# Eight tokens of each partition in one stored row: x blocks that step over a pair of chunks

## The chip, the core and the metric

The kernel runs on one core of a Trainium2 chip. The core has a matrix engine (PE), a vector engine (DVE), an activation engine (ACT), a general engine (POOL) and an engine that only issues transfers (SP); 16 DMA engines carry the traffic between HBM and the on-chip memory SBUF. The metric is device time in microseconds (us). The kernel before took 203.31 us, the median of two runs (203.01 and 203.61).

## What is computed

A linear recurrence runs along each of 8 sequences of 6400 tokens, 128 features wide; its output x is then put through a mixture of rank-16 adapters with two of eight experts chosen for each token. All in float32:

```python
# a, b: (8, 6400, 128); w_gate (128, 8); A (8, 128, 16); B (8, 16, 128)
for t in range(S):
    h = a[:, t] * h + b[:, t]
    x[:, t] = h
x = x.reshape(51200, 128)
logits = x @ w_gate
w = softmax(two largest logits of each token)
delta[n] = sum over the two experts e of w[n, e] * ((x[n] @ A[e]) @ B[e])
out = x + delta
```

## The kernel before

The 51,200 tokens are cut into 100 chunks of 512. The features lie along the 128 partitions while the recurrence runs, the tokens while loading, gating and storing.

**Front, for each chunk.** Loads of a and b bring two chunks at a time (512 KB, tiles `a_tm` and `b_tm`), eight tokens in a row of 4 KB in each partition; only the first four chunks are loaded one by one. Of such a pair, partitions 0 to 63 hold the first chunk, 64 to 127 the second. PE transposes them into `pA` and `pB` (line 728), groups of 16 small matmuls called `P`; ACT copies `pA` to `a_st` (L746); DVE runs the recurrence over the chunk with one scan instruction (L784) and writes x in half precision into a slot of `xT`, features by 512 tokens. There are NX = 24 slots, used in turn.

**Logits and adapters.** A block is 128 tokens. Four blocks make a chunk: block j of a chunk holds its columns j, j+4, j+8 and so on, which `xblock` (L665) gives as a view of the slot, so that the token of partition p and block j is token 4p + j of the chunk. Units of six blocks, one and a half chunks, (of four at the head and the tail; 69 in all) go through PE at L804: each block of x is loaded as the weights, and the gate and all A stream past it, into `pZ`. ACT copies a unit to `zl` (L810). A group of up to four units is gated on DVE and POOL (L841 to L880).

**Back, for each chunk.** POOL (for a few chunks DVE) multiplies the adapter inputs by the gate (L913), PE transposes the product (L926), ACT or DVE copies it to `zwT` (L932, L935), and PE adds x and the adapters' output in PSUM: L940 loads a block of x as weights and multiplies by the identity, L941 adds the product with B. These eight matmuls are the op `D`. ACT or DVE copies the result into `outt` (L955, L952), a ring of 72 blocks.

**Stores.** Two chunks at a time go out as one transfer of 512 KB (L986): each partition sends two rows of 2 KB, four tokens of the one chunk and four of the other. The last four chunks are stored one by one. The store that begins with chunk 68 is issued in two pieces, 124 partitions and 4.

**What sets the order.** Every piece of work is an op with an engine, a list of ops that it depends on, and a place. `schedule` (L330) puts the ops of each engine in order of a rank, made of a base and a number written out by hand for each op (`NUDGE`, L30). With `WINDOW` at 0 for each engine only the first op of its queue can be next, so the ranks are the order. `waits` (L400) turns the dependencies into semaphore waits ahead of the instructions. An engine carries out its list as it stands, and one that waits holds up all behind it.

The dependencies that the change touches: the logits op of a unit depends on the scan of the chunk in which its last block lies (`c1`, L797 and L807); the scan of a chunk depends on the last reader of its slot of `xT`, the op `D` of chunk c - 24 (`xlast`, L792 and L945); the fronts needed by a unit are created before it (L1020).

Of the kernel before, what the change touches and what calls it, by code (L numbers as in the profile page):

```python
# [8 lines left out]
F16 = mybir.dt.float16  # L9
# [226 lines left out]
NX = 24  # L236
# [207 lines left out]
def bass_associative_scan_2x2__then__mixture_of_adapters_kernel(  # L444
# [13 lines left out]
    C = 512  # L458
    J = C // 128
# [10 lines left out]
    b0 = 0  # L470
# [4 lines left out]
    NU = len(units)  # L475

    GMAX = 4
    stores = []
    c0 = 0
    for n in [2] * ((NCH - sum(STORE_TAIL)) // 2) + STORE_TAIL:  # L480
        stores.append((c0, n))
        c0 += n
    assert c0 == NCH

# [33 lines left out]
    with ExitStack() as stack:  # L518
        sb = stack.enter_context

        def sbuf(name, shape, dt, n=None):
            if n is None:
                return sb(nc.sbuf_tensor(name, shape, dt))
            return [sb(nc.sbuf_tensor(f"{name}{i}", shape, dt)) for i in range(n)]
# [20 lines left out]
        a_tm = sbuf("a_tm", [128, HC * J, D], F32, NL)  # L545
        b_tm = sbuf("b_tm", [128, HC * J, D], F32, NL)
        a_st = sbuf("a_st", [128, C], F32, NA)
        xT = sbuf("xT", [128, C], F16, NX)
        zl = sbuf("zl", [128, NZ, W], F32)
        zw = sbuf("zw", [128, J, 128], F16, NW)  # L550
        zwT = sbuf("zwT", [128, C], F16, NW)
        outt = sbuf("outt", [128, NO, 128], F32)
# [23 lines left out]
        def dma_sem(key):  # L576
            if key not in s_dma:
# [7 lines left out]
                out=ident_f[:, :], in_=ident_f[:, :], compare_op=ALU.not_equal, fill=1.0,  # L585
# [32 lines left out]
        def place_pick():  # L618
            with nc.allow_low_precision(reason="sums of a single one"):
# [8 lines left out]
                out=own[:, :], in_=ident_f[:, :].rearrange("q (e h) -> q e h", e=E),  # L628
# [6 lines left out]
                out=spread[:, :, :].rearrange("q l (e r) -> q l e r", e=E),  # L635
# [19 lines left out]
        o_Z, o_ze, o_mu, o_T, o_te, o_D, o_oe, o_st = {}, {}, {}, {}, {}, {}, {}, {}  # L655
        o_g = {}
        zlast, xlast, olast = {}, {}, {}

        def get(d, k):
            return [(d[k], True)] if k in d else []  # L660

        def xcols(c):
            return xT[c % NX][:, :]

        def xblock(b):  # L665
            return xcols(b // J).rearrange("d (p j) -> d j p", j=J)[:, b % J, :]

        def te_act(c):
            return c in TE_ACT
# [1 line left out]
        def fr(c, kind):  # L671
            if c < HEAD:
                return (EARLY + 2 * c + (kind == "B"), "", 0)
            return (PERIOD * (c // PERIOD), kind, c % PERIOD)
# [14 lines left out]
        def woven(c):  # L689
            return HEAD <= c < NCH - TAIL and c // HC not in FLAT  # L690
# [32 lines left out]
        def trans(*which):  # L723
            def f():
                lists = [pieces(*w) for w in which]
                for group in zip(*lists):
                    for args in group:
                        last = eng["pe"].transpose(*args)  # L728
                return last
            return f  # L730

        def part_a(c):
            return (c, a_tm, pA[:, c % 2, :])
# [4 lines left out]
        def deps_a(c):  # L738
            return [(o_la[c], True), (o_id, True)] + get(o_ae, c - 2)
# [8 lines left out]
        def front(c):  # L748
            r0 = rows[c]
            o_fi = []  # L750
            for k in range(FILL.get(c, 0)):
                o_fi.append((P.add(
                    "pe", f"fi{c}_{k}", 0.109, [(o_id, True)] + get(o_sc, c - 2),
                    lambda: eng["pe"].transpose(pB[:, c % 2, 0:128], ident_f[:, :], ident_f[:, :]), fr(c, "fi")), True))
            if not woven(c):
                o_A[c] = P.add("pe", f"A{c}", 0.109 * J, deps_a(c), trans(part_a(c)), fr(c, "A"))
                o_B[c] = P.add("pe", f"B{c}", 0.109 * J, deps_b(c) + o_fi, trans(part_b(c)), fr(c, "B"))
                add_ae(c)
            elif c % 2 == 0:
                if c not in o_A:  # L760
                    o_A[c] = P.add("pe", f"A{c}", HALVES, deps_a(c), trans(part_a(c)), fr(c, "A"))
                    add_ae(c)
                o_A[c + 1] = o_B[c] = P.add("pe", f"P{c}", HALVES, deps_a(c + 1) + deps_b(c) + o_fi,
                                            trans(part_a(c + 1), part_b(c)), fr(c, "B"))
                add_ae(c + 1)
            elif woven(c + 1):
                load_next(c + 1)
                o_A[c + 1] = o_B[c] = P.add("pe", f"P{c}", HALVES, deps_b(c) + deps_a(c + 1) + o_fi,
                                            trans(part_b(c), part_a(c + 1)), fr(c, "B"))
                add_ae(c + 1)  # L770
            else:
                o_B[c] = P.add("pe", f"B{c}", HALVES, deps_b(c) + o_fi, trans(part_b(c)), fr(c, "B"))

            x = xcols(c)
            starts = sorted({0} | {n * S - r0 for n in range(NB) if 0 < n * S - r0 < C})
            segs = list(zip(starts, starts[1:] + [C]))

            def scan():
                for s0, s1 in segs:
                    if (r0 + s0) % S == 0:  # L780
                        init = 0.0
                    else:
                        init = xcols(c - 1)[:, C - 1 : C]
                    last = eng["dve"].tensor_tensor_scan(  # L784
                        out=x[:, s0:s1], data0=a_st[c % NA][:, s0:s1], data1=pB[:, c % 2, s0:s1],
                        initial=init, op0=ALU.mult, op1=ALU.add,
                    )
                return last

            o_sc[c] = P.add("dve", f"sc{c}", 1.276 + 0.16 * (len(segs) - 1),  # L790
                            [(o_ae[c], True), (o_B[c], True)] + get(o_sc, c - 1)
                            + get(xlast, c % NX),  # L792
                            scan, fr(c, "sc"))

        def zlogits(u):
            b0, n = units[u]
            c1 = (b0 + n - 1) // J  # L797
            zb = zpos[u]
            zold = {zlast[zb + k].i: zlast[zb + k] for k in range(n) if zb + k in zlast}

            def zmm():
                for k in range(n):
                    o = k % (n // 2) * W
                    last = eng["pe"].matmul(pZ[:, k // (n // 2), o : o + W], xblock(b0 + k), Awg_h)  # L804
                return last

            o_Z[u] = P.add("pe", f"Z{u}", 0.11 + 0.059 * n, [(o_sc[c1], True), (o_ch, True), (o_cc, True)] + get(o_ze, u - 1), zmm, un(u, "Z"))  # L807

            def ze():
                return eng["act"].copy(  # L810
                    zl[:, zb : zb + n, :].rearrange("p (h k) w -> p h (k w)", h=2),
                    pZ[:, :, 0 : n // 2 * W])

            o_ze[u] = P.add("act", f"ze{u}", 0.167 + 0.1133 * n, [(o_Z[u], True)] + [(x, True) for x in zold.values()], ze, un(u, "ze"))
# [84 lines left out]
        def back_part(gi, ch, c, b0, n):  # L899
# [42 lines left out]
                return last  # L942

            o_D[c] = P.add("pe", f"D{c}", 0.11 + 0.112 * n, [(o_te[c], True)], delta, ba(gi, c, "D"))
            xlast[ch % NX] = o_D[c]  # L945
            o0 = b0 % NO
            freed = {olast[o0 + k].i: olast[o0 + k] for k in range(n) if o0 + k in olast}
            deps = [(o_D[c], True)] + [(x, True) for x in freed.values()]
# [27 lines left out]
        def store(c, m):  # L976
            q = c * J % NO
            r0 = rows[c]
            src = {olast[q + k].i: olast[q + k] for k in range(m * J)}
            dst = out[r0 : r0 + m * C, :].rearrange("(h p j) d -> p h j d", p=128, j=J)  # L980
            view = outt[:, q : q + m * J, :].rearrange("p (h j) d -> p h j d", j=J)
            cuts = SPLIT.get(c, [128])
            lows = [sum(cuts[:i]) for i in range(len(cuts))]

            def send():
                all = [eng["sp"].dma_start(dst[p : p + n], view[p : p + n]) for p, n in zip(lows, cuts)]  # L986
                return all if len(all) > 1 else all[0]

            op = P.add(
                "sp", f"st{c}", m * C * D * 4 / (STORE_RATE if m == 2 else LOAD_RATE), [(x, True) for x in src.values()],  # L990
                send, (PERIOD * (c // PERIOD), "st", c % PERIOD // 2),
                sem=dma_sem(f"st{q // (2 * J)}" if m == 2 else f"stx{c % 4}"), parts=len(cuts),
            )
            o_st[c] = op
            for k in range(m * J):
                olast[q + k] = op
# [17 lines left out]
                load(c, 1 if c < HEAD else HC)  # L1014

        nf, nb = 0, 0
        for gi, (u0, n) in enumerate(groups):
            for u in range(u0, u0 + n):
                b0, m = units[u]
                while nf * J < b0 + m:  # L1020
                    load_next(nf)
                    front(nf)
                    nf += 1
                zlogits(u)
            gating(gi)
            while (nb + 1) * J <= sum(units[u0 + n - 1]):
                while nb >= NCH - TAIL_CHUNKS and nf < NCH:
                    load_next(nf)
                    front(nf)
                    nf += 1  # L1030
                back(gi, nb)
                nb += 1
# [72 lines left out]
```

## Time and profile before

| | |
|---|---|
| median of the runs | 203.31 us |
| span of the profiled execution, first to last instruction | 200.9 us |
| moved by DMA | 79.26 MB at 395 GB/s, 29065 packets |
| scans on DVE (L784) | 104, of which 96 take 120.4 us |
| logits matmuls on PE (L804) | 400, mean 225 ns |
| x matmuls of the back (L940) | 400 (368 into pO, 16 into pA, 16 into pB) |
| pair stores | 47 of 512 KB, one of 496 KB and 16 KB |

The profile is one execution, recorded on the chip; its own time is known as the span, 200.9 us, which leaves out what lies before the first and after the last instruction. "Busy" is the time in which an engine carried out instructions. Matmuls overlap, and each lasts some 220 ns in the records while the next starts after some 55, so PE's busy time is not a measure of its rate. PEld is the weight loads of PE, which lie beside its matmuls. In groups of instructions a row gives the line, engine and operation, the output and inputs with their shapes, the count, the busy us and the mean ns of one, and then the idle time just before with what ended it. In lists of waits a row says who waited for whom: total us, times, longest. In lists in order of time a row begins with the start and the duration in us.

### The profile page before, as it was taken

The page shows a single profiled execution, that of the slowest core. Times are in us where ns is not written, and L with a number is a line of the kernel's source. Part 1 is how long each engine was busy: PE and PEld are TensorE (multiplying, and loading weights), DVE is VectorE, ACT ScalarE, POOL GpSimd, SP SyncE. Part 2 cuts the span into 40 slices and gives each one's busy share as a digit, 9 for nine tenths or more (in the row PEclk, how much of TensorE's full clock was granted, in tenths as well). Part 3 has the DMA queues.
Part 4 walks back from the last instruction along what each step waited for, and adds up shares of the span by engine and source line. Part 5 has one row for each costly group of instructions (what it writes and reads, how often), then busy time and mean ns, then how long its engine had stood idle before and what let it go on. Part 6 is the DMA issues. An engine that isn't in the chain of part 4 may idle for free.

```text
span 200.9 us, 7611 instructions
## 1 busy us (share of the span) xinstructions
PE 177.7 (88%) x3192; PEld 155.9 (78%) x3192; DVE 176.2 (88%) x283; ACT 175.8 (88%) x327; POOL 136.9 (68%) x176
## 2 busy tenths in 40 slices
PE   6888978999899969999988999899999997898970
PEld 6766867888688858888878888787888886787860
DVE  1699999999999968999897999798899998999971
ACT  2589998999779969999997999899999998899970
POOL 1331559498989887797987797868876466767420
PEclk9999999999999999999999999999999999999998
DMA  6999999999999999999999999999999999999985
GB/s 216 378 412 408 411 405 401 411 406 404 414 409 400 412 416 409 401 417 407 409 413 409 410 409 412 413 410 411 417 408 410 414 410 409 406 381 387 357 338 215
DMA packets 29065, 79.26 MB, mean 395 GB/s; under 512 B 2664, under 2 KB 2920, under 8 KB 29032
## 3 DMA queue, kind: packets, MB, share of 16 engines
q1 hardware_dynamic: 28456, 78.39, 99.0%
q8 instruction: 25, 0.41, 0.8%
q10 hardware_dynamic: 576, 0.40, 0.7%
q14 instruction: 8, 0.07, 0.1%
HBM read 52.56 MB, written 26.21 MB: 392 GB/s over the span
## 4 chain that ended last, share of the span: by engine, by line
DMA 33%; PE 27%; DVE 16%; ACT 15%; SPq 5%; issue 2%; DVEq 0%; ACTq 0%
DMA a_tm<-in_a_dram 26%; DVE xT L784 9%; DMA out_dram<-outt 7%; ACT zl L810 5%; PE pZ L804 5%; SPq L707 5%; PE pB L728 5%; PE pA L728 5%; ACT outt L955 4%; PE pO L940 4%; PE pO L926 4%; ACT a_st L746 4%; PE pO L941 3%; DVE zwT L935 2%; ACT zwT L932 2%
## 5 line engine op out<-in xcount | busy, mean ns | idle before, releaser
L784 DVE TENSOR_TENSOR_SCAN xT<-a_st,xT,pB 128x512 f16<-128x512 f32 x96 | 120.4, 1254 | 7.1 <-PE pA L728 4.3
L913 POOL TENSOR_TENSOR zw<-zl,g 128x512 f16<-128x512 f32 x88 | 92.7, 1067 | 27.9 <-DVE g L880 19.6
L728 PE MATMUL pB<-ident_f,b_tm 64*128 64x64 f32 (+1 forms) x784 | 69.3, 229 | 6.8 <-DMA a_tm<-in_a_dram 6.7
L728 PE MATMUL pA<-ident_f,a_tm 64*128 64x64 f32 (+1 forms) x784 | 69.8, 230 | 0.5 <-DMA b_tm<-in_b_dram 0.3
L746 ACT COPY a_st<-pA 128x512 f32<-128x512 f32 x100 | 63.3, 638 | 4.1 <-PE pA L728 3.3
L728 PEld LDWEIGHTS pB<-ident_f,b_tm 64*128 64x128 f32 (+1 forms) x784 | 56.4, 139 | 11.8 <-DMA a_tm<-in_a_dram 8.3
L810 ACT COPY zl<-pZ 128x816 f32<-128x816 f32 (+1 forms) x69 | 59.7, 865 | 2.0 <-PE pZ L804 1.7
L728 PEld LDWEIGHTS pA<-ident_f,a_tm 64*128 64x128 f32 (+1 forms) x784 | 56.8, 139 | 5.6 <-issue 0.4
L955 ACT COPY outt<-pO 128x512 f32<-128x512 f32 x88 | 55.9, 640 | 3.9 <-PE pO L941 3.0
L940 PE MATMUL pO<-ident_h,xT 128*128 128x128 f16 x368 | 51.6, 222 | 1.3 <-ACT zwT L932 1.0
L941 PE MATMUL pO<-cst_h,zwT 128*128 128x128 f16 x368 | 50.5, 219 | 0.0
L940 PEld LDWEIGHTS pO<-ident_h,xT 128*128 128x128 f16 x368 | 40.2, 113 | 4.3 <-ACT zwT L932 1.4
L804 PE MATMUL pZ<-cst_h,xT 128*128 128x136 f16 x400 | 35.9, 225 | 4.9 <-DVE xT L784 2.0
L941 PEld LDWEIGHTS pO<-cst_h,zwT 128*128 128x128 f16 x368 | 36.8, 100 | 0.0
L926 PE MATMUL pO<-ident_h,zw 128*128 128x128 f16 x368 | 35.2, 220 | 1.4 <-ACT outt L955 1.1
L804 PEld LDWEIGHTS pZ<-cst_h,xT 128*128 128x128 f16 x400 | 26.3, 114 | 9.1 <-DVE xT L784 4.3
L926 PEld LDWEIGHTS pO<-ident_h,zw 128*128 128x128 f16 x368 | 22.9, 97 | 4.7 <-ACT outt L955 1.3
L935 DVE COPY zwT<-pO 128x512 f16<-128x512 f16 x57 | 22.9, 407 | 4.0 <-PE pO L926 3.7
L932 ACT COPY zwT<-pO 128x512 f16<-128x512 f16 x35 | 21.9, 630 | 4.7 <-PE pO L926 4.3
L850 POOL TENSOR_TENSOR L<-k,m 128x192 f32<-128x192 f32 (+2 forms) x16 | 8.4, 524 | 6.2 <-DVE m L848 6.1
L872 POOL TENSOR_TENSOR k<-k,L 128x192 f32<-128x192 f32 (+1 forms) x17 | 9.4, 556 | 4.3 <-DVE L L868 3.0
L846 POOL TENSOR_TENSOR L<-L,k 128x192 f32<-128x192 f32 (+1 forms) x15 | 8.6, 576 | 5.4 <-DVE L L843 4.7
(58 smaller groups left out, 112.2 us busy)
## 6 DMA issues: line engine op xcount, KB each, us to landing
a_tm<-in_a_dram SPq DMA_DIRECT2D x48, 512.0 KB, 13.3
b_tm<-in_b_dram SPq DMA_DIRECT2D x48, 512.0 KB, 13.5
out_dram<-outt SPq DMA_DIRECT2D x47, 512.0 KB, 13.4
a_tm<-in_a_dram SPq DMA_DIRECT2D x4, 256.0 KB, 4.3
out_dram<-outt SPq DMA_DIRECT2D x4, 256.0 KB, 3.6
b_tm<-in_b_dram SPq DMA_DIRECT2D x3, 256.0 KB, 5.1
out_dram<-outt SPq DMA_DIRECT2D x1, 496.0 KB
b_tm<-in_b_dram ACTq DMA_DIRECT2D x1, 256.0 KB, 3.4
```

Of the source, the lines that this page charges most:

```text
L728: last = eng["pe"].transpose(*args)
L746: lambda: eng["act"].copy(a_st[c % NA][:, :], pA[:, c % 2, :]), fr(c, "ae"))
L784: last = eng["dve"].tensor_tensor_scan(out=x[:, s0:s1], data0=a_st[c % NA][:, s0:s1], data1=pB[:, c % 2, s0:s1], initial=init, op0=ALU.mul ...
L804: last = eng["pe"].matmul(pZ[:, k // (n // 2), o : o + W], xblock(b0 + k), Awg_h)
L810: return eng["act"].copy(zl[:, zb : zb + n, :].rearrange("p (h k) w -> p h (k w)", h=2), pZ[:, :, 0 : n // 2 * W])
L913: lambda: eng["pool"].tensor_tensor(out=wv, in0=zv, in1=gv, op=ALU.mult), ba(gi, c, "mu"))
L926: last = eng["pe"].transpose(ptile[:, k * 128 : k * 128 + 128], zz[:, k, :], ident_h[:, :])
L932: lambda: eng["act"].copy(zt, ptile[:, 0 : n * 128]), ba(gi, c, "ta"))
L935: lambda: eng["dve"].tensor_copy(zt, ptile[:, 0 : n * 128]), ba(gi, c, "te"))
L940: eng["pe"].matmul(dst, xblock(b0 + k), ident_h[:, :], start=True, stop=False)
L941: last = eng["pe"].matmul(dst, zt[:, k * 128 : k * 128 + 128], B_h, start=False, stop=True)
L955: lambda: eng["act"].copy(ov, bv), ba(gi, c, "oe"))
```

## The change

Stores of two chunks write one row of eight tokens in each partition: token 8p + k of the pair of chunks, 1024 tokens, is now in partition p and block k of the pair, for k from 0 to 7. So a block takes every eighth column of the two slots of the pair instead of every fourth of one. To make such a view possible the slots of `xT` become one tensor, and `tile_of` records which chunks are stored together. The last four chunks, stored singly, keep their blocks as they were. Since a block now has tokens of both chunks, the logits op of a unit depends on the scan of the last chunk of the pair in which the unit ends; the slots of a pair are free again when both `D` of the pair are done; and the fronts of a whole pair are created before the unit that needs them. The numbers of `NUDGE` are the same.

```diff
-    stores = []
+    stores, tile_of = [], {}
     c0 = 0
     for n in [2] * ((NCH - sum(STORE_TAIL)) // 2) + STORE_TAIL:
         stores.append((c0, n))
+        assert c0 % NX + n <= NX
+        for c in range(c0, c0 + n):
+            tile_of[c] = (c0, n)
         c0 += n
...
-        xT = sbuf("xT", [128, C], F16, NX)
+        xT = sbuf("xT", [128, NX * C], F16)
...
         def xcols(c):
-            return xT[c % NX][:, :]
+            o = c % NX * C
+            return xT[:, o : o + C]
 
         def xblock(b):
-            return xcols(b // J).rearrange("d (p j) -> d j p", j=J)[:, b % J, :]
+            s0, n = tile_of[b // J]
+            o = s0 % NX * C
+            return xT[:, o : o + n * C].rearrange("d (p j) -> d j p", p=128)[:, b - s0 * J, :]
...
                             [(o_ae[c], True), (o_B[c], True)] + get(o_sc, c - 1)
-                            + get(xlast, c % NX),
+                            + xlast.get(c % NX, (0, []))[1],
...
         def zlogits(u):
             b0, n = units[u]
-            c1 = (b0 + n - 1) // J
+            c1 = sum(tile_of[(b0 + n - 1) // J]) - 1
...
-            xlast[ch % NX] = o_D[c]
+            s0, m = tile_of[ch]
+            for k in range(s0, s0 + m):
+                if xlast.get(k % NX, (None, []))[0] != s0:
+                    xlast[k % NX] = (s0, [])
+                xlast[k % NX][1].append((o_D[c], True))
...
-            dst = out[r0 : r0 + m * C, :].rearrange("(h p j) d -> p h j d", p=128, j=J)
-            view = outt[:, q : q + m * J, :].rearrange("p (h j) d -> p h j d", j=J)
+            dst = out[r0 : r0 + m * C, :].rearrange("(p j) d -> p j d", p=128)
+            view = outt[:, q : q + m * J, :]
...
+        def fronts(c):
+            s0, n = tile_of[c]
+            return s0 + n
...
-                while nf * J < b0 + m:
+                while nf < fronts((b0 + m - 1) // J):
                     load_next(nf)
                     front(nf)
                     nf += 1
```

## The prediction

> **What bounds the kernel now.** I read the page's totals first, then stages, then the list of waits, then the instructions in order of time.
>
> ```profile
> span 200.9 us, 7611 instructions
> PE 177.7 (88%) x3192; PEld 155.9 (78%) x3192; DVE 176.2 (88%) x283; ACT 175.8 (88%) x327; POOL 136.9 (68%) x176
> q1 hardware_dynamic: 28456, 78.39, 99.0%
> DMA 33%; PE 27%; DVE 16%; ACT 15%; SPq 5%; issue 2%; DVEq 0%; ACTq 0%
> ```
>
> The DMA queue is busy through the whole span, and three engines follow at 88%. The chain of waits (last line) hops among all of them, so no resource has much room. The stages say how much:
>
> ```profile
> 20.00:180.00 160.00, 147.98 (x2783) 129.86 (x2782) 148.04 (x210) 149.09 (x274) 123.91 (x150) 1.00 1.03 409
> 80.00:100.00 20.00, 19.67 (x381) 17.58 (x380) 18.95 (x28) 19.76 (x39) 16.98 (x21) 1.00 1.04 409
> ```
>
> Columns: stage, its length, busy us of PE, weight loads, DVE, ACT, POOL, granted clock, DMA share, GB/s. From 20 to 180 us PE idles 160.0 - 148.0 = 12.0 us; from 80 to 100 us it idles 0.3. The waits that matter on PE:
>
> ```profile
> PE pB L728 <- DMA a_tm<-in_a_dram: 6.7, 10, 2.0
> PE pZ L804 <- DVE xT L784: 2.0, 5, 0.6
> ```
>
> So of the 12.0 idle us, 6.7 are waits for loads, which is what a kernel bound by DMA looks like from PE. DMA sets the pace, and PE, whose matmuls start in the kernel's own order all through the trace, is the next limit, 7% behind (12.0 of 160).
>
> **The change, part by part.**
>
> *The stores.* The 48 pair stores (the page has 47 whole and one cut in two) go from 256 rows of 2 KB to 128 rows of 4 KB: 6144 packets fewer. Two stretches price a packet, one with loads of 4 KB alone (12 to 32 us), one with stores of 2 KB alone (179 to 189 us):
>
> ```profile
> q1 hardware_dynamic: 2232, 8.12, 101.8%
> q1 hardware_dynamic: 1944, 3.74, 97.9%
> ```
>
> 8.12 MB in 4 KB rows are 1982 packets: 1.018 x 16 x 20 us / 1982 = 164 ns. 3.74 MB in 2 KB rows are 1826: 0.979 x 16 x 10 / 1826 = 85.8 ns, or 172 for 4 KB (the rest of each count are tiny completion packets, about 1% of the time, left in both). The saving is at most 6144 x (172 - 164) / 16 = 3.1 us of every DMA engine. It may be 0, since the queue moves 409 GB/s with stores mixed in against 8.12 MB / 20 us = 406 without. [...] I take 0, because the next part makes compute slower than DMA; 0 to -3.1 stay as bounds.
>
> *The wait for the second chunk.* Block b of a pair now takes every eighth column of 1024, so its columns lie in both chunks. The logits matmuls (L804) of a unit must wait for the scan of the second chunk of the pair in which the unit ends. Of 69 units, 33 end in a first chunk (chunk 0 to 94, even) and wait for one scan more; the others wait as before. Orders stay, so PE stands still there. These units come in two kinds. The first, in order of time:
>
> ```profile
> 101.14 1.27 DVE L784 TENSOR_TENSOR_SCAN xT<-a_st,xT,pB 128x512 f16<-128x512 f32 x1
> ...
> 102.60 0.22 PE L728 MATMUL pA<-ident_f,a_tm 64*128 64x64 f32 x1
> ...
> 102.75 0.55 PE L804 MATMUL pZ<-cst_h,xT 128*128 128x136 f16 x6
> ...
> 102.91 1.27 DVE L784 TENSOR_TENSOR_SCAN xT<-a_st,xT,pB 128x512 f16<-128x512 f32 x1
> ...
> 103.90 0.27 PE L728 MATMUL pA<-ident_f,a_tm 64*128 64x64 f32 x1
> ...
> 104.66 1.28 DVE L784 TENSOR_TENSOR_SCAN xT<-a_st,xT,pB 128x512 f16<-128x512 f32 x1
> ```
>
> The unit at 102.75 ends in chunk 56, scanned by 102.41. Now it needs chunk 57, whose transposes come just ahead of it on PE (last one at 102.60) and whose scan ends at 102.91 + 1.27 = 104.18. With 0.05 us for the signal it starts at 104.23: PE waits 1.48 us. Behind it on PE queue the deltas and transposes of older chunks and the transposes at 103.90, which feed the scan at 104.66; behind its result, ACT's copy to zl, the gating, POOL's product, the stores. All move by the wait. The other kind:
>
> ```profile
> 116.17 1.28 DVE L784 TENSOR_TENSOR_SCAN xT<-a_st,xT,pB 128x512 f16<-128x512 f32 x1
> ...
> 116.40 0.22 PE L728 MATMUL pA<-ident_f,a_tm 64*128 64x64 f32 x1
> ...
> 117.50 0.54 PE L804 MATMUL pZ<-cst_h,xT 128*128 128x136 f16 x6
> 117.54 1.28 DVE L784 TENSOR_TENSOR_SCAN xT<-a_st,xT,pB 128x512 f16<-128x512 f32 x1
> ```
>
> Here the unit starts at the end of its scan, 117.45; the next ends at 118.82, so it waits 1.37. For all 33 units I took (end of the second chunk's scan + 0.05 - start of the unit), where above zero; first and last of the 33:
>
> ```profile
> 7.54 1.28 DVE L784 TENSOR_TENSOR_SCAN xT<-a_st,xT,pB 128x512 f16<-128x512 f32 x1
> 8.31 0.28 PE L804 MATMUL pZ<-cst_h,xT 128*128 128x136 f16 x2 [0.45 <-ACT cst_h L651]
> ...
> 172.22 1.28 DVE L784 TENSOR_TENSOR_SCAN xT<-a_st,xT,pB 128x512 f16<-128x512 f32 x1
> 172.97 0.40 PE L804 MATMUL pZ<-cst_h,xT 128*128 128x136 f16 x4
> ```
>
> 0.56 and 0.58 us at these ends, 1.2 to 1.7 in most of the middle, 36.4 in sum. What takes some of it back is PE's idle time: the 6.7 us of waiting for loads go, as loads run on while PE stands; of the other 5.3, waits for engines that are pushed back too, I count half. Net: 36.4 - 6.7 - 2.7 = **+27.0 us**. Bounds: nothing absorbed, +36.4; for the low end the second kind counts only from its own chunk's transposes, because DVE may use PE's pauses to catch up (116.40 + 0.22 + 0.05 + 1.28 + 0.05 - 117.50 = 0.50 instead of 1.37). The 33 then sum to 25.7, and with all 12.0 idle us absorbed +13.7. I take the upper reading of the waits, because the first chunk's scan itself follows transposes that the wait before has delayed.
>
> *The step of the x loads.* 96 paired chunks x 4 blocks x 2 uses (L804, L940) = 768 weight loads read columns 16 bytes apart instead of 8.
>
> ```profile
> L940 PEld LDWEIGHTS pO<-ident_h,xT 128*128 128x128 f16 x368 | 40.2, 113 | 4.3 <-ACT zwT L932 1.4 <-DVE zwT L935 0.6
> L941 PEld LDWEIGHTS pO<-cst_h,zwT 128*128 128x128 f16 x368 | 36.8, 100 | 0.0
> L728 PEld LDWEIGHTS pA<-ident_f,a_tm 64*128 64x128 f32 (+1 forms) x784 | 56.8, 139 | 5.6 <-issue 0.4 <-DMA b_tm<-in_b_dram 0.4
> ```
>
> ```profile
> 103.19 0.22 PE L941 MATMUL pO<-cst_h,zwT 128*128 128x128 f16 x1
> 103.25 0.22 PE L940 MATMUL pO<-ident_h,xT 128*128 128x128 f16 x1
> 103.30 0.22 PE L941 MATMUL pO<-cst_h,zwT 128*128 128x128 f16 x1
> ...
> 104.14 0.22 PE L728 MATMUL pA<-ident_f,a_tm 64*128 64x64 f32 x1
> 104.14 0.22 PE L728 MATMUL pB<-ident_f,b_tm 64*128 64x64 f32 x1
> 104.20 0.22 PE L728 MATMUL pA<-ident_f,a_tm 64*128 64x64 f32 x1
> ```
>
> A step of 8 bytes already makes the load 13 ns longer than a packed one, and the matmuls still follow each other at 0.055 us, so it is hidden under the matmul before. The longest load here, 139 ns, goes with a spacing of 0.06. I take 2 ns on each of 768, +1.5 us; bounds 0 and 6 x 768 = 4.6.
>
> *The rest.* A slot of xT comes free only when both chunks' deltas are done. The nearest case, chunk 36's scan against chunk 13's last delta:
>
> ```profile
> 54.04 0.22 PE L941 MATMUL pO<-cst_h,zwT 128*128 128x128 f16 x1
> 65.00 1.28 DVE L784 TENSOR_TENSOR_SCAN xT<-a_st,xT,pB 128x512 f16<-128x512 f32 x1
> ```
>
> 10.7 us of cover, and both sides move together: 0. The stores keep their waits and their place on SP, and issue half the descriptors: 0.
>
> The sum for the profiled execution: 200.9 + 27.0 + 1.5 = 229.4 us of span. The runs shown have a median of 203.3, 2.4 above the span, so 203.3 + 28.5 = **232 us**.
>
> **The rivals.**
>
> - *DVE catches up and every idle moment is used*: +13.7, so 217. For it: DVE idles 160 - 148.0 = 12 us too and has room once PE pauses. Against: its scans need PE's transposes.
> - *Nothing is absorbed*: 203.3 + 36.4 + 4.6 = 244.3. For it: stages such as 80 to 100 us, with 0.3 us idle. Against: the loads surely run ahead.
> - *The x loads show*: if the full 139 - 113 = 26 ns come out in the spacing, 768 x 26 = 20.0 us on top of the main case, 252. [...] Against: the step of 8 bytes moved the spacing by nothing.
> - *Not slower*: DMA decides after all. If PE can lose these pauses without the loads noticing, only the packets count: 203.3 - 3.1 = 200.2. For it: the queue's 99.0%, and loads issued far ahead. It decides only while the pauses stay below PE's 12.0 idle us; the low reading has 25.7. That the orders do not stay, so that the units slip behind other work on PE, would end here too.
>
> **How the numbers follow.** Main case 0.58 (232, its own range 224 to 240), DVE catching up 0.16, nothing absorbed 0.10, loads showing 0.07, not slower 0.09. A range of 212 to 245 leaves out the loads' case, the not-slower case and a little of the ends. About 2% (4 us) is what a measurement of this kernel can tell from no change. The first four cases are all slower: 0.91. The last is split: 0.06 within 2%, 0.03 faster by more, if the mixed queue gains beyond 3.1 us.
>
> **What would show it.** The wait of L804 on DVE's scan, 2.0 us now, should grow to 25 us or more in some 30 waits of about 1.4 us. PE's wait for a_tm should fall from 6.7 towards 0, and the DMA queue should fall to about 86% (99.0 x 200.9 / 229.4 = 86.7, and some store time less). The x loads' mean shows the third term: 113 still, or about 140. q1 should count some 6100 packets fewer. I am wrong if the wait on the scan stays under 10 us, if its pauses lie on PE without the end moving, or if L804 and L940 no longer follow at 0.055 to 0.062 us.

## The result: 243.2 us, and where the 40 us are

| | before | changed |
|---|---|---|
| median of 2 runs | 203.31 us | 243.23 us (242.13 and 244.33) |
| span of the profiled execution | 200.9 us | 240.3 us |
| PE busy | 177.7 us | 190.0 us |
| PE idle (span less busy) | 23.2 us | 50.3 us |
| wait of the logits matmuls for the scan | 2.0 us in 5 waits | 41.3 us in 31 waits |

The ratio is 1.196, 95% interval 1.183 to 1.210: slower. All intervals here leave out runs over 1.5% above the fastest of their kernel: two of wait_only, one of changed_again and one of tolerant_orders_b (205.41 us).

In the changed kernel the lines stand lower by six: the scan is L790, the transposes L734, the logits L810 with their copy at L816, the x and adapter matmuls of the back L946 and L947. Its page, totals first:

```profile
span 240.3 us, 7587 instructions
PE 190.0 (79%) x3192; PEld 167.9 (70%) x3192; DVE 178.2 (74%) x283; ACT 181.9 (76%) x327; POOL 137.5 (57%) x176
PEclk9988795899979999999999999999999999999998
q1 hardware_dynamic: 22312, 78.39, 86.8%
DVE 31%; PE 30%; ACT 9%; POOL 2%; issue 2%; DVEq 0%
```

DMA led the chain of waits before, with 33%. Now it isn't in it: scans and matmuls alternate, and the queue is busy 86.8% of a longer span. DVE's busy time grew by 2.0 us, POOL's by 0.6 and ACT's by 6.1; all three are busy for a smaller share of the span than PE and stand still more. PE has the growth on both sides: 50.3 - 23.2 = 27.1 us idle, 190.0 - 177.7 = 12.3 us busy, together the 39.4 us of the span. The list of waits (who for whom: total us, times, longest) names the first part:

```profile
PEld pZ L810 <- DVE xT L790: 46.3, 32, 2.4
PE pZ L810 <- DVE xT L790: 41.3, 31, 2.2
POOL zw L919 <- PE pO L932: 35.5, 27, 3.9
ACT zl L816 <- PE pZ L810: 34.7, 31, 2.0
...
PEld pA L734 <- DMA a_tm<-in_a_dram: 0.2, 1, 0.2
```

PE's second row is the new wait; ACT's and POOL's are the same pause one and two steps on, so they are not added to it. PE's wait for a_tm, 6.7 us before, is gone. In order of time such a wait looks like this (start and duration in us; a group of instructions in one row has xN):

```profile
118.77 2.65 DVE L790 TENSOR_TENSOR_SCAN xT<-a_st,xT,pB 128x512 f16<-128x512 f32 x2
...
119.40 0.23 PE L946 MATMUL pO<-ident_h,xT 128*128 128x128 f16 x1
...
119.47 0.22 PE L947 MATMUL pO<-cst_h,zwT 128*128 128x128 f16 x1
...
119.52 0.23 PE L946 MATMUL pO<-ident_h,xT 128*128 128x128 f16 x1
...
119.83 0.22 PE L947 MATMUL pO<-cst_h,zwT 128*128 128x128 f16 x1
...
121.48 0.60 PE L810 MATMUL pZ<-cst_h,xT 128*128 128x136 f16 x6 [1.43 <-DVE xT L790]
...
122.12 0.84 ACT L816 COPY zl<-pZ 128x816 f32<-128x816 f32 x1 [0.91 <-PE pZ L810]
```

The scans of both chunks of a pair run back to back and end at 118.77 + 2.65 = 121.42. PE is done at 120.05 and stands until 121.48, 1.43 us; ACT waits for the unit in turn.

The second part, 12.3 us of busy time for the same matmuls, shows in two places. The first is the x loads, as a group:

```profile
L946 PEld LDWEIGHTS pO<-ident_h,xT 128*128 128x128 f16 x368 | 46.9, 145 | 3.5 <-ACT zwT L938 0.8 <-DVE zwT L941 0.5
```

They take 145 ns against 113. In order of time above, an x matmul and its adapter matmul take 119.52 - 119.40 = 0.12 us, where the pair at 103.19 and 103.30 of the kernel before took 0.11. The other is PE's clock, by stretches of 3.41 us (columns as in the prediction; the granted clock is the third figure from the end):

```profile
6.30:9.71 3.41, 1.93 (x22) 1.74 (x21) 2.62 (x3) 0.85 (x2) 0.97 (x1) 1.00 1.03 403
9.71:13.12 3.41, 3.33 (x44) 3.15 (x45) 2.35 (x9) 2.46 (x6) 0.63 (x2) 1.00 1.02 417
13.12:16.54 3.42, 1.65 (x35) 1.27 (x30) 3.29 (x4) 2.52 (x5) 0.98 (x2) 1.00 1.03 412
16.54:19.95 3.41, 3.10 (x34) 2.79 (x35) 1.45 (x3) 1.53 (x3) 0.32 (x1) 0.50 1.03 405
...
23.36:26.77 3.41, 1.89 (x40) 1.51 (x38) 2.08 (x4) 1.98 (x4) 2.08 (x2) 1.00 1.03 410
26.77:30.19 3.42, 3.42 (x47) 2.99 (x46) 2.59 (x5) 2.61 (x6) 1.11 (x2) 0.50 1.03 407
...
33.60:37.01 3.41, 1.88 (x32) 1.64 (x34) 2.62 (x3) 2.12 (x6) 1.99 (x2) 1.00 1.03 414
37.01:40.43 3.42, 2.45 (x36) 1.95 (x34) 2.52 (x3) 1.97 (x3) 2.12 (x3) 0.50 1.03 410
40.43:43.84 3.41, 3.00 (x42) 2.80 (x42) 1.36 (x3) 1.42 (x2) 1.59 (x2) 0.50 0.74 288
...
64.32:67.73 3.41, 1.17 (x24) 0.93 (x23) 2.37 (x3) 1.42 (x3) 2.75 (x4) 1.00 0.89 240
67.73:71.14 3.41, 3.41 (x45) 2.98 (x40) 1.92 (x4) 1.57 (x3) 1.06 (x2) 0.50 0.91 315
71.14:74.56 3.42, 3.22 (x56) 2.88 (x54) 3.04 (x5) 2.51 (x5) 3.42 (x5) 1.00 1.01 412
```

In five of these stretches, 17.1 us in all, PE ran at half its clock. Each of them, or the first of two in a row, follows a stretch in which PE was busy for 1.65, 1.89, 1.88 or 1.17 us of 3.41. After 1.93 (first row) the clock stayed full, and late in the span it stayed full after less:

```profile
180.40:183.81 3.41, 1.83 (x38) 1.52 (x34) 3.35 (x5) 2.16 (x4) 2.08 (x2) 1.00 0.94 351
183.81:187.22 3.41, 3.24 (x62) 2.90 (x62) 1.85 (x3) 2.64 (x5) 0.97 (x2) 1.00 0.93 356
```

So where pauses add up to some 1.5 us or more of a stretch, the next one can run at half clock, and the pauses then cost a second time: the matmuls after them take longer (L947 311 ns in the stretches from 26.77 and 67.73 us, 219 from 80 to 230 us, at 1.00). Between 1.8 and 1.9 us busy this trace has both outcomes. The kernel before had no stretch at half from 20 to 180 us, where its clock was 1.00.

### The profile page after: what moved, and what is told of

The parts are those of the page before. It is cut to its first block, busy times and chain, and to the rows that moved or that the text cites. A ratio compares the mean times of both kernels' runs of the same rounds, so it can differ in the third digit from the quotient of the medians.

```text
span 240.3 us, 7587 instructions
## 1 busy us (share of the span) xinstructions
PE 190.0 (79%) x3192; PEld 167.9 (70%) x3192; DVE 178.2 (74%) x283; ACT 181.9 (76%) x327; POOL 137.5 (57%) x176
## 3 DMA queue, kind: packets, MB, share of 16 engines
q1 hardware_dynamic: 22312, 78.39, 86.8%
## 4 chain that ended last, share of the span: by engine, by line
DVE 31%; PE 30%; ACT 9%; POOL 2%; issue 2%; DVEq 0%
DVE xT L790 23%; PE pZ L810 7%; PE pA L734 6%; PE pO L946 5%; PE pO L947 4%; PE pO L932 4%; ACT outt L965 3%; ACT zl L816 3%; PE pB L734 3%; DVE zwT L941 2%; ACT a_st L752 2%; DVE zw L923 2%; DVE g L886 2%; POOL zw L919 1%; DVE outt L962 1%
## 5 line engine op out<-in xcount | busy, mean ns | idle before, releaser
L790 DVE TENSOR_TENSOR_SCAN xT<-a_st,xT,pB 128x512 f16<-128x512 f32 x96 | 120.5, 1256 | 15.1 <-PE pB L734 9.3
L816 ACT COPY zl<-pZ 128x816 f32<-128x816 f32 (+1 forms) x69 | 56.8, 823 | 35.0 <-PE pZ L810 34.7
L810 PE MATMUL pZ<-cst_h,xT 128*128 128x136 f16 x400 | 39.8, 236 | 42.7 <-DVE xT L790 41.3
L734 PE MATMUL pA<-ident_f,a_tm 64*128 64x64 f32 (+1 forms) x784 | 71.6, 236 | 0.1
L734 PE MATMUL pB<-ident_f,b_tm 64*128 64x64 f32 (+1 forms) x784 | 71.3, 236 | 0.0
L810 PEld LDWEIGHTS pZ<-cst_h,xT 128*128 128x128 f16 x400 | 31.2, 147 | 49.0 <-DVE xT L790 46.3
L752 ACT COPY a_st<-pA 128x512 f32<-128x512 f32 x100 | 59.6, 601 | 6.8 <-PE pA L734 4.0
L734 PEld LDWEIGHTS pA<-ident_f,a_tm 64*128 64x128 f32 (+1 forms) x784 | 58.8, 145 | 5.3 <-issue 0.8
L734 PEld LDWEIGHTS pB<-ident_f,b_tm 64*128 64x128 f32 (+1 forms) x784 | 58.8, 145 | 3.7 <-issue 0.4
L965 ACT COPY outt<-pO 128x512 f32<-128x512 f32 x88 | 52.0, 596 | 7.5 <-PE pO L947 6.8
L946 PE MATMUL pO<-ident_h,xT 128*128 128x128 f16 x368 | 56.4, 235 | 0.7 <-ACT zwT L938 0.5
L947 PE MATMUL pO<-cst_h,zwT 128*128 128x128 f16 x368 | 54.1, 222 | 0.0
L946 PEld LDWEIGHTS pO<-ident_h,xT 128*128 128x128 f16 x368 | 46.9, 145 | 3.5 <-ACT zwT L938 0.8
L947 PEld LDWEIGHTS pO<-cst_h,zwT 128*128 128x128 f16 x368 | 40.2, 109 | 0.0
L941 DVE COPY zwT<-pO 128x512 f16<-128x512 f16 x57 | 23.4, 415 | 20.2 <-PE pO L932 20.1
L865 DVE TENSOR_REDUCE m<-zl 128x24 f32<-128x192 f32 (+2 forms) x17 | 5.6, 330 | 12.5 <-ACT zl L816 12.5
```

What stands on the lines that cost most here:

```text
L752: lambda: eng["act"].copy(a_st[c % NA][:, :], pA[:, c % 2, :]), fr(c, "ae"))
L790: last = eng["dve"].tensor_tensor_scan(out=x[:, s0:s1], data0=a_st[c % NA][:, s0:s1], data1=pB[:, c % 2, s0:s1], initial=init, op0=ALU.mul ...
L816: return eng["act"].copy(zl[:, zb : zb + n, :].rearrange("p (h k) w -> p h (k w)", h=2), pZ[:, :, 0 : n // 2 * W])
L941: lambda: eng["dve"].tensor_copy(zt, ptile[:, 0 : n * 128]), ba(gi, c, "te"))
L946: eng["pe"].matmul(dst, xblock(b0 + k), ident_h[:, :], start=True, stop=False)
L947: last = eng["pe"].matmul(dst, zt[:, k * 128 : k * 128 + 128], B_h, start=False, stop=True)
```

## The experiments

The theory after the result: the new dependency, under unchanged orders, makes PE wait, and that is some 30 us; the longer x loads and the halved clock are the remaining 10. The rivals: the longer loads are the main cost by way of PE's pace; the longer rows are; or the blocks over two chunks cost this much in whatever order.

**wait_only.** The kernel before, with the new dependency of the logits and nothing else: blocks, loads and rows stay.

```diff
             c1 = (b0 + n - 1) // J
+            c1 = c1 if c1 >= NCH - sum(STORE_TAIL) else c1 | 1
...
+        def fronts(c):
+            return c + 1 if c >= NCH - sum(STORE_TAIL) else (c | 1) + 1
...
-                while nf * J < b0 + m:
+                while nf < fronts((b0 + m - 1) // J):
```

> The kernel before with one edit: the logits of a unit wait for the scan of the second chunk of the pair; blocks of x keep their step of 8 bytes, stores their rows of 2 KB. Theory (the wait makes the idle time, and the pauses let the granted clock fall): PE waits some 41 us for the scan, the mean granted clock falls to about 0.96 as in the changed kernel, x loads stay at 113 ns; 243.2 less about 5 us of longer x loads, so 234 to 240 us. Rival (the x loads' step of 16 bytes is the larger part, and makes the clock fall): under 225 us, clock at 0.99 or more.

Measured: 237.56, 233.90, 238.89 and 235.85 us, with mean clocks of 0.966, 0.989, 0.968 and 0.981, against 202.58; the ratio by the second and the fourth is 1.159 (1.152 to 1.165). Page, x loads and waits of the profiled run, the first:

```profile
span 235.8 us, 7587 instructions
PE 182.8 (78%) x3192; PEld 159.8 (68%) x3192; DVE 177.1 (75%) x283; ACT 180.5 (77%) x327; POOL 137.3 (58%) x176
```

```profile
L941 PEld LDWEIGHTS pO<-ident_h,xT 128*128 128x128 f16 x368 | 41.1, 115 | 3.9 <-ACT zwT L933 0.9 <-DVE zwT L936 0.7
```

```profile
PE pZ L805 <- DVE xT L784: 41.8, 31, 2.3
```

The whole wait of the changed kernel is here, with x loads of 115 ns, not 145. The best run, at clock 0.989, is 31.3 us over before: the wait makes more than three quarters of the loss. PE's busy time grew too, 182.8 - 177.7 = 5.1 us, without the step of 16 bytes. In this execution, at a mean clock of 0.966, four stretches of 3.41 us ran at half (the first from 25.34 us), and most of the 5.1 us is theirs, by the price of a stretch under changed_again.

**step_only.** The waits, orders and rows of before, but logits and deltas read their x from the pair of chunks before, at a step of 16 bytes. It adds up x of other tokens, so its output is that of another computation of the same size.

```diff
+        xT = sbuf("xT", [128, NX * C], F16)
...
         def xblock(b):
-            return xcols(b // J).rearrange("d (p j) -> d j p", j=J)[:, b % J, :]
+            s0, n = pair_read(b // J)
+            o = s0 % NX * C
+            return xT[:, o : o + n * C].rearrange("d (p j) -> d j p", p=128)[:, b % (n * J), :]
+
+        def pair_read(c):
+            if c < 2 or c >= NCH - sum(STORE_TAIL):
+                return c, 1
+            return (c & ~1) - 2, 2
```

> The kernel before, but the logits and the deltas of a pair of chunks read the x of the pair before it, whose scans are long done, at a step of 16 bytes (so x of another token enters logits, adapters and sum); waits, orders and stores of 2 KB as before. Theory: x loads 143 ns, the matmul after them 4 to 9 ns later, about 5 us of PE time, most of it in the 12 us that PE idles: 203 to 206 us, clock 0.99 or more. Rival (the step is the larger part): 212 us or more.

Measured: 202.59 us against 202.58, ratio 1.000 (0.999 to 1.001), just under the 203 to 206 us of the theory. Its page, groups and waits:

```profile
PE 183.4 (91%) x3192; PEld 162.6 (81%) x3192; DVE 177.1 (88%) x283; ACT 177.1 (88%) x327; POOL 136.8 (68%) x176
```

```profile
L948 PEld LDWEIGHTS pO<-ident_h,xT 128*128 128x128 f16 x368 | 46.2, 143 | 4.2 <-ACT zwT L940 1.6 <-DVE zwT L943 0.5
```

```profile
PE pB L736 <- DMA a_tm<-in_a_dram: 2.1, 3, 0.9
```

The loads take 143 ns and PE 5.7 us more, and the end doesn't move: PE's wait for a_tm shrank from 6.7 to 2.1 us in exchange. In this kernel, where DMA sets the pace, the step costs no time. That says nothing yet of a kernel in which PE does.

**rows_only.** Only the store is changed: the two lines of `dst` and `view` of the diff. The blocks stay, so the tokens of a pair come out in another order.

> The kernel before with only the stores' rows changed to 4 KB (tokens within a pair land in other rows of the output); blocks, waits and orders as before. If the packets' saving of up to 3.1 us reaches the end: 200.2 to 202 us, verdict faster by about 1%. If the mixed queue hides it, or compute is as late as the loads: 203.3, the same within 0.3%.

Measured: 201.64 us against 202.58, ratio 0.9945 (0.9928 to 0.9961). From its page:

```profile
span 199.8 us, 7611 instructions
q1 hardware_dynamic: 22312, 78.39, 97.9%
```

The packets fall by the 6144 that were counted, and the end comes 0.94 us sooner: this is what the rows can bring here, of 3.1 at most by the estimated price of a packet.

**window_orders.** The changed kernel, with `schedule` free to take any op that can start within a few us instead of the first of its queue.

```diff
-WINDOW = {'pe': 0.0, 'act': 0.0, 'dve': 0.0, 'pool': 0.0, 'sp': 0.0}
+WINDOW = {'pe': 3.0, 'act': 4.0, 'dve': 4.0, 'pool': 0.0, 'sp': 0.0}
```

> The changed kernel with orders adapted: the scheduler may take an op ahead of its rank within 3 us on PE and 4 us on ACT and DVE, so other work can stand where PE waited. Theory (the fixed orders cost the time): PE's wait for the scan falls under 8 us, clock 0.99, x loads still 143 ns, 204 to 213 us. Rival (the step of 16 bytes costs the time): 225 us or more whatever the order.

Measured: 204.96 us (204.86 to 205.05), ratio 1.011 (1.009 to 1.013). Page and waits:

```profile
PE 186.2 (92%) x3192; PEld 163.9 (81%) x3192; DVE 176.8 (87%) x283; ACT 177.9 (88%) x327; POOL 136.5 (67%) x176
PEclk9999999999999999999999999999999999999998
q1 hardware_dynamic: 22312, 78.39, 96.4%
```

```profile
PE pZ L810 <- DVE xT L790: 2.6, 5, 0.7
```

Same blocks, same loads, same dependency, and 38 of the 40 us are gone: the wait is back at 2.6 us, the clock at 0.996 to 0.997, the queue at 96.4%. The dependency costs only by what stands still behind it.

**changed_again, fill_changed, fill_wait.** The changed kernel once more; the same with 16 matmuls of the identity by itself ahead of each waiting unit from 3 to 60 (29 units, 464 matmuls), which keep PE busy in the wait and add nothing to the result; and wait_only with the same filler.

```diff
+            if 3 <= u <= 60 and c1 != (b0 + n - 1) // J:
+                NUDGE[f"fz{u}"] = NUDGE[f"Z{u}"] - 1e-4
+
+                def fill():
+                    for k in range(16):
+                        last = eng["pe"].matmul(pZ[:, 0, 0:128], ident_h[:, :], ident_h[:, :])
+                    return last
+
+                P.add("pe", f"fz{u}", 0.9, [(o_ih, True)] + get(o_ze, u - 1), fill, un(u, "Z"))
```

> The changed kernel as it is, beside the two that follow, so that times and granted clocks can be compared on one chip. 240 to 245 us, mean clock 0.95 to 0.98.

> The changed kernel, with 16 idle matmuls of the identity (about 0.9 us) ahead of each waiting unit of logits from unit 3 to 60, so that PE has work in the pauses. Theory (the pauses let the granted clock halve for 3.4 us at a time, and that costs time): clock 0.99 or more, 233 to 239 us, although PE carries out 464 matmuls more. Rival (the halved clock falls into waiting time and costs nothing, or the clock falls for another reason): as changed_again or up to 3 us above it.

> The kernel of wait_only (step of 8 bytes, rows of 2 KB, the longer wait) with the same idle matmuls. Both fill kernels have the full clock, so fill_changed less this one is what the step of 16 bytes costs where PE sets the pace, apart from the rows. Theory: clock 0.99 or more, 229 to 234 us, 3 to 6 us under fill_changed. Rival (the step is hidden here as it was in step_only): within 1.5 us of fill_changed.

Measured: changed_again 239.53, 239.71, 243.00 and 245.96 us at clocks of 0.983, 0.981, 0.958 and 0.937. So one program differs by 6.4 us with its clock, some 1.4 us for a hundredth. Two profiled executions of this program show where the time goes: that of the result, 240.3 us with five stretches at half, and that of changed_again, 237.7 us with two. Page, waits and the two stretches of the latter:

```profile
span 237.7 us, 7587 instructions
PE 187.3 (79%) x3192; PEld 165.9 (70%) x3192; DVE 178.3 (75%) x283; ACT 181.6 (76%) x327; POOL 137.3 (58%) x176
```

```profile
PE pZ L810 <- DVE xT L790: 41.4, 31, 2.2
```

```profile
24.64:28.06 3.42, 3.42 (x46) 2.99 (x46) 2.26 (x3) 2.71 (x5) 0.77 (x2) 0.50 1.03 411
65.60:69.02 3.42, 3.42 (x41) 3.11 (x39) 2.66 (x5) 1.12 (x3) 1.80 (x2) 0.50 1.01 411
```

The 5th and the 23rd of the 104 scans, first in the slower execution, then in this one:

```profile
14.13 1.28 DVE L790 TENSOR_TENSOR_SCAN xT<-a_st,xT,pB 128x512 f16<-128x512 f32 x1
...
48.79 1.27 DVE L790 TENSOR_TENSOR_SCAN xT<-a_st,xT,pB 128x512 f16<-128x512 f32 x1
```

```profile
14.31 1.28 DVE L790 TENSOR_TENSOR_SCAN xT<-a_st,xT,pB 128x512 f16<-128x512 f32 x1
...
46.22 1.27 DVE L790 TENSOR_TENSOR_SCAN xT<-a_st,xT,pB 128x512 f16<-128x512 f32 x1
```

PE's waits for the scan are alike (41.3 and 41.4 us), and so is its idle time (50.3 and 237.7 - 187.3 = 50.4). The busy time differs by 2.7 us and the span by 2.6. The slower execution is 0.18 us ahead at the 5th scan and 2.57 behind at the 23rd; between them it has four stretches at half, the other one. After that each has one more, at nearly the same work, and the distance stays: at the 101st scan it is 215.15 - 212.56 = 2.59. So the distance grows only where the clocks differ, and three stretches more cost 2.57 + 0.18 = 2.75 us, some 0.9 us each.

fill_changed takes 241.09 us at 0.987 to 0.998, fill_wait 236.14 at 0.988 to 0.995. The waits of both:

```profile
PE pZ L810 <- DVE xT L790: 17.0, 27, 1.7
```

```profile
PE pZ L805 <- DVE xT L784: 16.8, 27, 1.8
```

The filler covers some 24 us of the wait and holds the clock up, but does not bring the time under that of the better runs without it. Both kernels miss what the theory expected (233 to 239 us and 229 to 234), and fill_changed lies where its rival had it. The filler delays something itself: fill_wait at 0.99 is 2.2 us over wait_only's best run at 0.989. So as a test in time of what the clock costs, fill_changed is inconclusive. The pair of them answers another question, since filler, clock and waits are alike: 241.09 - 236.14 = 5.0 us is the price of the changed blocks, rows among them, where PE sets the pace. Without filler, at the same clock of 0.981, changed_again's 239.71 us and wait_only's 235.85 are 3.9 us apart. There the longer loads aren't free.

**new_orders, before_new_orders.** All five orders written out anew by a search over a planner's times, in place of the ranks: for the changed kernel and, as a control, for the one before.

```diff
-            rank[op.i] = op.base + (TEMPLATE[op.kind][op.k] if op.kind in TEMPLATE else 0.0) + NUDGE.get(op.name, 0.0)
+            rank[op.i] = place[op.eng, op.name]
```

> The changed kernel with the order of every engine written anew by a search that knows the longer wait, the loads of 143 ns and the stores' shorter time. Theory (the change is worth its 0.9 us once the orders hide the wait and the step): 200.5 to 203 us, PE's wait for the scan under 5 us, clock 0.99. Rival (what the wait and the step cost cannot be hidden, since PE is then busy over 90%): 204 us or more, no better than window_orders.

> A control: the kernel before, rows of 2 KB and blocks within a chunk, with its orders written anew by the same search. If new orders alone give a gain, this is as fast as new_orders or faster; if the rows of 4 KB give it, this stays at 202.6 us, within 0.4%.

Measured: 204.37 us (ratio 1.0075, 1.0043 to 1.0107) and 203.31 us (1.0022, 1.0003 to 1.0042) against 202.88. The first misses its 200.5 to 203. The control shows that this search gives the kernel before nothing, so what it gives the changed kernel is not a gain that any kernel would have had.

**tolerant_orders_a, tolerant_orders_b.** As new_orders, with orders searched for under scattered times.

> The changed kernel once more with all orders written anew, as in new_orders, but each engine's head (about 2 to 20 us) is kept as in window_orders, and the search now weighs orders by their end under scattered load and instruction times instead of one fixed set. Theory (the time of the change is an order that waits, nothing else, and what was left in new_orders came from orders too tight for the chip's scatter): no wait of L810 on the scan over 3 us in sum, 199 to 202.5 us, level with before (202.6 to 202.9) or up to 1.5% under it, the 0.94 us of the longer rows among it. Rival (the blocks over two chunks need some 1 to 2% whatever the orders, since PE carries 5.7 us more of loads): 203.5 to 206 again, with PE busy over 92% of the span.

> As tolerant_orders_a, another result of the same search (another start of its head). Same numbers: 199 to 202.5 us by the theory, 203.5 to 206 by the rival. If only one of the two lies under before, the orders are luck and not a version to keep.

Measured, against 202.70: 202.56 us (ratio 0.9984, 0.9972 to 0.9996) and 203.74 us (1.0033, 1.0005 to 1.0061). Page and waits of the first:

```profile
span 200.7 us, 7642 instructions
PE 185.1 (92%) x3192; PEld 163.9 (82%) x3192; DVE 175.7 (88%) x283; ACT 177.4 (88%) x327; POOL 138.1 (69%) x176
```

```profile
PE pZ L884 <- DVE xT L864: 2.9, 5, 1.3
```

The changed kernel can be as fast as the one before, and the rival (1 to 2% whatever the orders) falls with a. But a lies 0.06 us over the theory's range, 199 to 202.5, and b over before, so by the rule set beforehand this is luck with an order and no version to keep. The kernel before was not searched for in this second way. By the ratios a is 0.8 us behind rows_only (0.9984 - 0.9945 of 202.7), so most of what the rows bring is lost again; PE's 7.4 us more of busy time leave its orders less room, which may be why, and wasn't tried by itself.

## Why the prediction was right, and where it was off

The prediction said slower, 232 us, 212 to 245. The changed kernel took 243.2: in the range, and 11 us over its middle. By its steps:

*The wait for the second chunk* was right, and so was its net. Gross it was put at 36.4 us, in some 30 waits of 1.4 us; the row grew by 41.3 - 2.0 = 39.3 in 31 waits of 1.33. The waits for loads were to give back 6.7 and gave 6.7 (the 0.2 us left are a weight load's, not a matmul's); the other idle time was to give 2.7, half of 5.3 by a guess, and by what is left gave 39.3 - 6.7 - 27.1 = 5.5. PE's idle time was to grow by 27.0 us and grew by 27.1. That it agrees to 0.1 us is luck: the waits came out 2.9 us larger, what they took back 2.8 us larger, and the two errors cancel. wait_only shows that it is this dependency alone, window_orders that it costs only by the unchanged order. That DVE would not catch up in the pauses, the reason for taking the upper reading, held in the wait that is shown in order of time: the scan that PE waits for starts right behind the one before it. DVE's waits for the transposes into pB grew too, from 4.5 us to 13.9.

*The step of the x loads* is the term of the sum that was mis-sized. It took 2 ns on each of 768 loads, +1.5 us, with 4.6 as its bound; busy time grew by 12.3. The load's own length came out as the rival "the x loads show" had it, about 140 ns (143 in step_only), and the spacing did not: not 26 ns of it, but 5.7 us / 768 = 7.4 ns. So the term is 3.9 to 5.0 us in time, with the rows in it, and 5.7 in busy time: at or over its bound of 4.6, which rested on a row of other shapes (139 ns beside a spacing of 0.06). Here one of the prediction's signs of being wrong came: the matmul behind an x matmul follows at 119.47 - 119.40 = 0.07 us, not at 0.055 to 0.062.

The rest of the busy time, 12.3 - 5.7 = 6.6 us, holds a term that the sum didn't have. Every duration was taken from rows with a clock of 1.00, and the sum let PE stand still for 1.4 us some thirty times without asking what its clock does then. Five stretches at 0.9 us each are some 4.5 us of the 6.6; no run shows the other 2 by themselves. wait_only has 5.1 us without the longer loads. In the rows of after the clock is at 0.50 or 1.00 for whole stretches of 3.41 us. No wait of PE on a scan was over 2.2 us, so no longer pause was needed for the clock to fall.

*The stores* were put at 0 because compute would be slower than DMA. That held, and rows_only shows what was there to gain, 0.94 us. The 3.1 us at most were an estimate from two stretches; the 1% of the time that it gives to the small packets (under 512 B, 249 of 2234 and 116 of 1945) no row shows. *The rest* at 0 held too: the list of waits of after has no scan that waits for a delta.

The rivals. *Nothing is absorbed* gave 244.3, nearest to the time, and is still wrong: it needed PE's idle time to grow by 36.4 us. The time alone would have picked it; idle and busy time apart tell them apart. *The x loads show* needed 20 us of spacing, and got 5.7. *DVE catches up* and *not slower* fall with the wait of 41.3 us and the queue's 86.8%, which was forecast at about 86.

The pieces in time: 31.3 us for the wait (wait_only at clock 0.989), 5.0 for the blocks (or 3.9), and 1.4 us for each hundredth of clock below 0.989. The two runs of the changed kernel had 0.961 and 0.958, 3 hundredths, 4 us. The sum is 40.3 (or 39.2), beside 39.9 measured. The clock's piece rests on runs and on two profiled executions of one program; no edit switched the half clock on and off without another cost.

## What to carry to other kernels

A dependency that is widened by one step costs nothing as work. Under an order that is written out it costs its wait times the number of ops that meet it, on the engine that waits in line, less the idle time that it takes the place of: here 41.8 us of waits cost 31.3 us of time. So count those ops and their slack in the trace of before, and move the orders with the change, or it will look like a bad change (1.196) when it is nearly an even one (0.998 to 1.011 in four sets of orders). And pauses of PE can have two prices: the time that it stands, and the clock of the matmuls behind them, here some 0.9 us for each stretch of 3.41 us at half clock. Before a layout is changed for longer rows, try the rows alone, with the tokens in another order: here the most to be had was 0.5%.

## What was not expected of the hardware

- The half clock came without a long pause: PE's longest wait on a scan was 2.2 us. Stretches of 3.41 us with PE busy for 1.17 to 1.89 us were followed by one at 0.50, stretches with 1.83 and 1.93 us by one at 1.00. In wait_only one with 1.75 us (from 62.89 us) was followed by full clock and one with 1.84 (from 21.93 us) by half. So the busy time of one stretch, as these rows count it, doesn't settle the clock of the next between some 1.75 and 1.9 us. At half clock, a stretch busy for 2.45 us was followed by another at half, one with 3.00 us by one at full.
- A weight load of 128 x 128 in half precision takes 100 ns packed (L941 before), 113 with columns 8 bytes apart (L940 before) and 143 with 16 (step_only). By the rows of before, the matmuls' spacing of some 55 ns hides the first 13 ns; of the next 30 it hides three quarters, 7.4 ns a load being left. Of the jump from 113 to 143 ns, nothing reached the end in step_only (202.59 us against 202.58).
